# Value loads of a block-attention and soft-MoE kernel: two transfers on 128 partitions in place of eight on 32, with one more GpSimd copy

## The chip, the cores and the metric

The kernel runs on one NeuronCore of a Trainium2 chip. The metric is the device time of one execution, in microseconds (us). Five engines run side by side, each its own list of instructions in order: PE (TensorE, matmuls and transposes), DVE (VectorE), ACT (ScalarE), POOL (GpSimd) and SP (SyncE). SP does no arithmetic here; it issues every transfer between the chip's main memory and the on-chip memory of 128 partitions. [...]

## What is computed

Attention inside chunks of 64 tokens for 8 images of 8 heads, then a soft mixture of experts over all 4608 tokens:

```python
scores = scale * q_c @ k_c.T                  # per image, head and chunk of 64 tokens
attn = softmax(scores)
x = (attn @ v_c) -> (4608, 512)               # q, k, v: (8, 8, 576, 64) float32

logits = x @ phi                              # phi (512, 32)
d = softmax over tokens; c = softmax over slots
slot_out[e] = relu((d.T @ x)[e] @ w1[e]) @ w2[e]   # 8 experts, w1 (512, 1024), w2 (1024, 512)
out = c @ slot_out
```

## The kernel before

The 4608 tokens are worked off in nine blocks of 512 tokens, and each block in four units of two heads, so there are 36 units, t = 0 to 35. Eight of the blocks are the first 512 tokens of one image. The ninth (`b == NB - 1`) gathers the last 64 tokens of all eight images; it is fifth in order, so its units are t = 16 to 19.

For each unit SP loads keys and queries (`load_qk`, one transfer of 256 KB each, in the ninth block two of 128 KB each) into one of three buffers (`kn`, `qn`), five units ahead. Values are loaded for two units at once, that is, four heads (`load_v`, called when t is even, for units t+2 and t+3), into one of two buffers `vna` and `vnb`; together they are 512 KB. Before, these 512 KB go as eight transfers of 64 KB, each to 32 partitions. The weights `w1` and `w2` of the experts are loaded meanwhile in pieces of 512 KB (`load_pieces`), a little over one for each unit from t = 2 on.

A key or value row pair (tokens 2i and 2i+1, 512 bytes) lands on one partition. The matmul `values` wants something else: 64 keys of a chunk on 64 partitions, in both halves of a 128-column product, so `spread_v` on POOL copies one row of each pair to the other 32 partitions (two copies for each half of the partitions, `w` = 0 and 1, on 32 partitions of 256 elements each), and a memset sets the column of ones that gives the softmax sum. The even chunk (m = 0) of a pair of chunks lies on partitions `lo`, the odd one (m = 1) on `hi`. The eight transfers put the even chunk's pairs into columns 0 to 127 and the odd chunk's into columns 64 to 191 of each head's 194.

The loop over t writes the order of every engine by hand. In iteration t: weight pieces; scores of unit t; `spread_v(t)` on POOL; `values(t-1)` on PE; `load_v(t+2)` for even t; transposes of the keys and queries of unit t+1 (`turn_qk`); on POOL the pairing of heads of unit t+2 (`pair_heads`, two copies on 128 partitions of 512 elements); `load_qk(t+5)`; transposes of the outputs of unit t-2, and the logits and other block work at some iterations; at its end the transposes of the probabilities. POOL therefore runs spread, pair, pair for one unit after another, and a wait in `spread_v(t)` also holds the pairing for unit t+2. After the loop come a short tail of the last block, the experts (`up`, `turn`, `down`), and the outputs (`combine`, `store`).

SP issues in the order of the code. Each transfer signals one of eight semaphores, taken in rotation (shown below as DMAHW0 to DMAHW7), and it waits until the transfer that had the same semaphore before, eight places back, has landed; so at most eight transfers are under way. It also waits until its buffer is free.

Of the kernel before, what the change touches and what calls it, by code (L numbers as in the profile page):

```python
# [15 lines left out]
def kernel(  # L16
# [10 lines left out]
    nc = tc.nc  # L27
# [3 lines left out]
    B, H, S, D = q.shape  # L31
# [5 lines left out]
    TB = 512  # L37
    NB = B * S // TB
# [69 lines left out]
    with ExitStack() as actx:  # L108
# [6 lines left out]
        def tiles(name, n, shape):  # L115
            return [st.tile(shape, F32, name=f"{name}{i}") for i in range(n)]
# [6 lines left out]
        vn = tiles("vna", 1, [P, 2, 4, VW])  # L123
# [21 lines left out]
        def unit(t):  # L145
            n, hp = divmod(t, NHP)
            return n, order_b[n], hp
# [15 lines left out]
        def load_v(t):  # L163


            n, b, hp = unit(t)
            hs = slice(2 * hp, 2 * hp + 4)
            if b < NB - 1:
                src = v[b, hs, 0:TB].rearrange("a (M w m i u) d -> M w m i a (u d)", M=2, w=2, m=2, u=2)
            else:  # L170
                src = v[:, hs, TB:S].rearrange("(M w m) a (i u) d -> M w m i a (u d)", M=2, w=2, u=2)
            for M in range(2):
                for w in range(2):
                    for m in range(2):
                        p0 = 64 * w + 32 * m
                        nc.sync.dma_start(vn[t // 2 % 2][p0:p0 + 32, M, :, D * m:D * (m + 2)], src[M, w, m])  # L176

        def values_of(t):
            return vn[t // 2 % 2][:, :, 2 * (t % 2):2 * (t % 2) + 2]

        def spread_v(t):


            vv = values_of(t)
            for w in range(2):
                lo, hi = slice(64 * w, 64 * w + 32), slice(64 * w + 32, 64 * w + 64)
                nc.gpsimd.tensor_copy(vv[hi, :, :, 0:D], vv[lo, :, :, D:2 * D])  # L187
                nc.gpsimd.tensor_copy(vv[lo, :, :, 2 * D:3 * D], vv[hi, :, :, D:2 * D])  # L188
            nc.gpsimd.memset(vv[:, :, :, D:D + 1], 1.0)  # L189

# [218 lines left out]
        load_qk(0)  # L409
        load_qk(1)  # L410
        load_v(0)
        load_qk(2)
        nc.sync.dma_start(phi_sb, phi.rearrange("(f p) s -> p f s", p=P))
# [16 lines left out]
        for t in range(NT + 1):  # L430
# [5 lines left out]
            if t < NT:  # L436
                scores(t)
                s_sub(t)
                spread_v(t)
# [3 lines left out]
            if t % 2 == 0 and t + 2 < NT:  # L443
                load_v(t + 2)
# [227 lines left out]
```

## Time and profile before

| what | value |
|---|---|
| time, median of 3 runs (lowest to highest) | 308.19 us (305.33 to 310.34) |
| time of the profiled execution | 304.26 us |
| its span, first to last instruction | 302.5 us |
| busy share of PE, POOL, ACT, DVE | 74%, 36%, 41%, 41% |
| 16 DMA engines, busy share over the span | 79.3% (the SP queue) |
| mean granted PE clock | 0.891 |
| packets of the SP queue | 61776 |

The profile comes from one execution. A wait is the idle time of an engine just ahead of an instruction, put down to what released it last. "SPq" is SP issuing transfers; where it issues eight in one merged row, the row's length holds the waits between them as well. The DMA share of a short stretch can stand above 1, since packets overlap. The profiled execution is 3.9 us below the median of the runs.

### The profile page before, as it was taken

The page shows a single profiled execution, that of the slowest core. Times are in us where ns is not written, and L with a number is a line of the kernel's source. Part 1 is how long each engine was busy: PE and PEld are TensorE (multiplying, and loading weights), DVE is VectorE, ACT ScalarE, POOL GpSimd, SP SyncE. Part 2 cuts the span into 40 slices and gives each one's busy share as a digit, 9 for nine tenths or more (in the row PEclk, how much of TensorE's full clock was granted, in tenths as well). Part 3 has the DMA queues.
Part 4 walks back from the last instruction along what each step waited for, and adds up shares of the span by engine and source line. Part 5 has one row for each costly group of instructions (what it writes and reads, how often), then busy time and mean ns, then how long its engine had stood idle before and what let it go on. Part 6 is the DMA issues. An engine that isn't in the chain of part 4 may idle for free.

```text
span 302.5 us, 9554 instructions
## 1 busy us (share of the span) xinstructions
PE 222.6 (74%) x3828; PEld 165.6 (55%) x3828; DVE 122.9 (41%) x303; ACT 125.0 (41%) x277; POOL 108.7 (36%) x279
## 2 busy tenths in 40 slices
PE   8787859667784874979647787489576799998910
PEld 8666747557563653858437666376443224645800
DVE  0355534452743444274361656247453101025720
ACT  1467526453471554346543565356441011024610
POOL 2854552625435172543707437347310300000000
PEclk9999977997996899588995999989997699998675
DMA  7877958678695877868879687888689399968997
GB/s 189 243 179 194 278 160 226 207 195 258 178 251 153 231 203 205 264 165 215 239 194 288 190 228 232 223 230 263 141 286 407 119 335 361 347 213 292 316 321 298
DMA packets 61819, 71.99 MB, mean 238 GB/s; under 512 B 5456, under 2 KB 52560, under 8 KB 61776
## 3 DMA queue, kind: packets, MB, share of 16 engines
q1 hardware_dynamic: 61776, 71.39, 79.3%
q8 instruction: 30, 0.49, 0.7%
q14 instruction: 13, 0.11, 0.1%
HBM read 61.93 MB, written 9.44 MB: 236 GB/s over the span
## 4 chain that ended last, share of the span: by engine, by line
DMA 54%; PE 23%; POOL 6%; issue 4%; SPq 3%; DVE 2%; ACT 2%; POOLq 0%; ACTq 0%; DVEq 0%
DMA w<-in_moe_w_dram 29%; DMA vnb<-in_v_dram 14%; DMA vna<-in_v_dram 7%; PE ph L537 5%; PE pf L598 5%; PE po L571 5%; DMA qn<-in_q_dram 2%; PE pav L258 2%; SPq L154 2%; DMA knb<-in_k_dram 1%; SPq L176 1%; POOL vnb L188 1%; POOL vna L188 1%; POOL vnb L187 1%; POOL vna L187 1%
## 5 line engine op out<-in xcount | busy, mean ns | idle before, releaser
L216 ACT COPY kT<-pg 128x512 f32<-128x512 f32 x36 | 21.1, 586 | 80.2 <-PE pg L197 80.2
L232 DVE TENSOR_REDUCE mx<-psc 128x8 f32<-128x512 f32 x36 | 24.8, 689 | 45.9 <-PE psc L226 45.8
L258 PE MATMUL pav<-vnb,at 64*64 64x65 f32 x576 | 16.4, 247 | 26.2 <-POOL vnb L189 10.1
L187 POOL COPY vnb<-vnb 32x256 f32<-32x256 f32 x36 | 14.2, 394 | 50.7 <-DMA vnb<-in_v_dram 49.2
L247 ACT COPY at<-pt 128x512 f32<-128x512 f32 x36 | 21.1, 585 | 26.0 <-PE pt L244 26.0
L187 POOL COPY vna<-vna 32x256 f32<-32x256 f32 x36 | 14.2, 393 | 47.1 <-DMA vna<-in_v_dram 45.6
L197 PE MATMUL pg<-ident,kp 128*128 128x128 f32 x144 | 26.4, 312 | 4.3 <-DVE eT L336 4.3
L226 PE MATMUL psc<-kT,qT 64*64 64x64 f32 x1152 | 26.3, 229 | 4.4 <-issue 3.7
L258 PEld LDWEIGHTS pav<-vnb,at 64*64 64x64 f32 x576 | 13.7, 153 | 28.6 <-POOL vnb L189 24.2
L244 PE MATMUL pt<-ident,sc 128*128 128x128 f32 x144 | 24.8, 297 | 4.5 <-ACT sc L238 3.6
L226 PEld LDWEIGHTS psc<-kT,qT 64*64 64x64 f32 x1152 | 21.1, 139 | 11.2 <-issue 8.0
L197 PE MATMUL ph<-ident,qp 128*128 128x128 f32 x144 | 25.1, 302 | 2.2 <-issue 2.2
L258 PE MATMUL pav<-vna,at 64*64 64x65 f32 x576 | 15.0, 236 | 15.6 <-POOL vna L189 9.4
L233 DVE TENSOR_TENSOR sc<-psc,mx 128x512 f32<-128x512 f32 x36 | 24.9, 692 | 3.2
L273 DVE TENSOR_TENSOR xb<-pav,rc 128x512 f32<-128x512 f32 x36 | 24.9, 691 | 1.2
L244 PEld LDWEIGHTS pt<-ident,sc 128*128 128x128 f32 x144 | 17.1, 151 | 14.9 <-ACT sc L238 7.3
L279 PE MATMUL px<-ident,xb 128*128 128x128 f32 x144 | 24.6, 299 | 0.0
L238 ACT ACTIVATE sc<-sc 128x512 f32<-128x512 f32 x36 | 22.8, 633 | 0.6 <-DVE sc L233 0.6
L258 PEld LDWEIGHTS pav<-vna,at 64*64 64x64 f32 x576 | 12.6, 143 | 17.9 <-POOL vna L189 15.2
L193 POOL COPY qp<-qn 128x512 f32<-128x512 f32 x36 | 21.9, 609 | 0.1
L216 ACT COPY qT<-ph 128x512 f32<-128x512 f32 x36 | 20.7, 576 | 1.7 <-PE ph L197 1.7
L197 PEld LDWEIGHTS pg<-ident,kp 128*128 128x128 f32 x144 | 17.2, 155 | 7.6 <-issue 4.9
(94 smaller groups left out, 347.5 us busy)
## 6 DMA issues: line engine op xcount, KB each, us to landing
w<-in_moe_w_dram SPq DMA_DIRECT2D x64, 512.0 KB, 8.1
qn<-in_q_dram SPq DMA_DIRECT2D x32, 256.0 KB, 4.9
knb<-in_k_dram SPq DMA_DIRECT2D x21, 256.0 KB, 4.9
vna<-in_v_dram SPq DMA_DIRECT2D x72, 64.0 KB, 5.0
vnb<-in_v_dram SPq DMA_DIRECT2D x72, 64.0 KB, 5.6
out_dram<-ob SPq DMA_DIRECT2D x8, 512.0 KB, 3.7
out_dram<-ob SPq DMA_DIRECT2D x4, 1024.0 KB, 7.9
kna<-in_k_dram SPq DMA_DIRECT2D x11, 256.0 KB, 3.1
```

What stands on the lines that cost most here:

```text
L187: nc.gpsimd.tensor_copy(vv[hi, :, :, 0:D], vv[lo, :, :, D:2 * D])
L193: nc.gpsimd.tensor_copy(dst.rearrange("p j a d -> p a j d"), src)
L197: nc.tensor.transpose(out=dst[:, P * j:P * (j + 1)], in_=(kp if isk else qp)[:, j].rearrange("p a d -> p (a d)"), identity=ident)
L216: nc.scalar.copy(o, i)
L226: nc.tensor.matmul(psc[CH * m:CH * (m + 1), a, o:o + CH], lhsT=qT[r, c], rhs=kT[r, c], start=True, stop=True)
L232: nc.vector.reduce_max(mx, pv, axis=AX.X)
L233: nc.vector.tensor_tensor(sc.rearrange("p a M (w x) -> p a (M w) x", x=CH), pv, mx.unsqueeze(3).to_broadcast([P, 2, 4, CH]), ALU.subtract)
L238: nc.scalar.activation(sc, sc, AF.Exp, scale=SCALE)
L244: nc.tensor.transpose(out=pt[:, o:o + P], in_=sc[:, a, M], identity=ident)
L258: nc.tensor.matmul(pvv[q_, 2 * w + M, a, 0:D + 1], lhsT=at[r, a, M, q_], rhs=values_of(t)[r, M, a, 2 * D * m:2 * D * m + D + 1], start=Tru ...
L273: nc.vector.tensor_tensor(x_of(t).rearrange("p l (a d) -> p l a d", d=D), pvv[:, :, :, 0:D], rc.to_broadcast([P, 4, 2, D]), ALU.mult)
L279: nc.tensor.transpose(out=px[:, P * l:P * (l + 1)], in_=x_of(t)[:, l], identity=ident)
```

## The change

`load_v` loads the 512 KB of two units by two transfers of 256 KB on all 128 partitions, one for each group M of 256 tokens, all into columns 64 to 191. In the ninth block it issues eight transfers of 64 KB on 128 partitions, one for each M and head, whose source runs over four images and then 32 row pairs. Since every pair now lies in columns 64 to 191, `spread_v` first copies columns 64 to 127 to columns 0 to 63 on all partitions, and then makes the four copies of before, of which the first of each half reads other columns.

```diff
-            if b < NB - 1:
-                src = v[b, hs, 0:TB].rearrange("a (M w m i u) d -> M w m i a (u d)", M=2, w=2, m=2, u=2)
-            else:
-                src = v[:, hs, TB:S].rearrange("(M w m) a (i u) d -> M w m i a (u d)", M=2, w=2, u=2)
             for M in range(2):
-                for w in range(2):
-                    for m in range(2):
-                        p0 = 64 * w + 32 * m
-                        nc.sync.dma_start(vn[t // 2 % 2][p0:p0 + 32, M, :, D * m:D * (m + 2)], src[M, w, m])
+                dst = vn[t // 2 % 2][:, M, :, D:3 * D]
+                if b < NB - 1:
+                    nc.sync.dma_start(dst, v[b, hs, TB // 2 * M:TB // 2 * (M + 1)].rearrange(
+                        "a (p u) d -> p a (u d)", u=2))
+                else:
+                    for a in range(4):
+                        nc.sync.dma_start(dst[:, a], v[4 * M:4 * (M + 1), 2 * hp + a, TB:S].rearrange(
+                            "c (i u) d -> c i (u d)", u=2))
...
             vv = values_of(t)
+            nc.gpsimd.tensor_copy(vv[:, :, :, 0:D], vv[:, :, :, D:2 * D])
             for w in range(2):
                 lo, hi = slice(64 * w, 64 * w + 32), slice(64 * w + 32, 64 * w + 64)
-                nc.gpsimd.tensor_copy(vv[hi, :, :, 0:D], vv[lo, :, :, D:2 * D])
+                nc.gpsimd.tensor_copy(vv[hi, :, :, 0:D], vv[lo, :, :, 2 * D:3 * D])
                 nc.gpsimd.tensor_copy(vv[lo, :, :, 2 * D:3 * D], vv[hi, :, :, D:2 * D])
             nc.gpsimd.memset(vv[:, :, :, D:D + 1], 1.0)
```

On SP, around the second load into `vnb` (units 6 and 7), the order before is this; L154 loads keys or queries, L103 a weight piece, L176 values, and the brackets name the semaphores that the transfer waits for:

```order
L103 DMA w_0_1_439<-in_moe_w_dram 128x1024 [waits DMAHW5_49]
L176 DMA vnb_94<-in_v_dram 32x4x128 [waits DMAHW6_49,PE_49]
L176 DMA vnb_94<-in_v_dram 32x4x128 [waits DMAHW7_49,PE_49]
L176 DMA vnb_94<-in_v_dram 32x4x128 [waits DMAHW0_49]
L176 DMA vnb_94<-in_v_dram 32x4x128 [waits DMAHW1_49,PE_49]
L176 DMA vnb_94<-in_v_dram 32x4x128 [waits DMAHW2_49,PE_49]
L176 DMA vnb_94<-in_v_dram 32x4x128 [waits DMAHW3_49,PE_49]
L176 DMA vnb_94<-in_v_dram 32x4x128 [waits DMAHW4_49]
L176 DMA vnb_94<-in_v_dram 32x4x128 [waits DMAHW5_49,PE_49]
L154 DMA kna_87<-in_k_dram 128x2x256 [waits DMAHW6_49,Pool_49]
L154 DMA qn_84<-in_q_dram 128x2x256 [waits DMAHW7_49,Pool_49]
```

Of the change, the same place on SP, from the weight piece ahead of the values to the next load of values, two units later:

```order
L103 DMA w_0_1_425<-in_moe_w_dram 128x1024 [waits DMAHW3_49]
L171 DMA vnb_94<-in_v_dram 128x4x128 [waits DMAHW4_49,PE_49]
L171 DMA vnb_94<-in_v_dram 128x4x128 [waits DMAHW5_49,PE_49]
L154 DMA kna_87<-in_k_dram 128x2x256 [waits DMAHW6_49,Pool_49]
L154 DMA qn_84<-in_q_dram 128x2x256 [waits DMAHW7_49,Pool_49]
L103 DMA w_0_1_425<-in_moe_w_dram 128x1024 [waits DMAHW0_49]
L154 DMA knb_98<-in_k_dram 128x2x256 [waits DMAHW1_49,Pool_49]
L154 DMA qn_85<-in_q_dram 128x2x256 [waits DMAHW2_49,Pool_49]
L103 DMA w_1_0_570<-in_moe_w_dram 128x1024 [waits DMAHW3_49]
L171 DMA vna_91<-in_v_dram 128x4x128 [waits DMAHW4_49,PE_49]
L171 DMA vna_91<-in_v_dram 128x4x128 [waits DMAHW5_49,PE_49]
```

Before, the last value transfer waits for the weight piece just ahead of the first. In the change two units issue eight transfers (two of values, two of keys, two of queries, two weight pieces), so a value transfer waits for the value transfer of two units earlier.

On POOL, the first unit of a pair before (L187 and L188 are the four copies, L193 the pairing of heads):

```order
L187 COPY vnb_94<-vnb_94 32x2x2x64 [waits DMAHW5_49,DMAHW1_49,Pool_49]
L188 COPY vnb_94<-vnb_94 32x2x2x64 [waits DMAHW6_49,DMAHW2_49]
L187 COPY vnb_94<-vnb_94 32x2x2x64 [waits DMAHW7_49,DMAHW3_49]
L188 COPY vnb_94<-vnb_94 32x2x2x64 [waits DMAHW4_49,DMAHW0_49]
L189 MEMSET vnb_94 128x2x2 [waits Pool_49]
L193 COPY kp<-knb_98 128x2x4x64 [waits PE_49]
```

and of the change (L185 is the new copy, L194 the pairing of heads):

```order
L185 COPY vnb_94<-vnb_94 128x2x2x64 [waits DMAHW6_49,DMAHW5_49]
L188 COPY vnb_94<-vnb_94 32x2x2x64 [waits Pool_49]
L189 COPY vnb_94<-vnb_94 32x2x2x64 [waits Pool_49]
L188 COPY vnb_94<-vnb_94 32x2x2x64
L189 COPY vnb_94<-vnb_94 32x2x2x64 [waits Pool_49]
L190 MEMSET vnb_94 128x2x2 [waits Pool_49]
L194 COPY kp<-knb_98 128x2x4x64 [waits DMAHW3_49,PE_49]
```

One copy on 128 partitions is added ahead of the four, which wait for it and partly for each other through POOL's own semaphore.

## Rows read from the trace of the kernel before

**Rows 1.** The page: chain that ended last, shares of the span by line

```profile
DMA w<-in_moe_w_dram 29%; DMA vnb<-in_v_dram 14%; DMA vna<-in_v_dram 7%; PE ph L537 5%; PE pf L598 5%; PE po L571 5%; DMA qn<-in_q_dram 2%; PE pav L258 2%; SPq L154 2%; DMA knb<-in_k_dram 1%; SPq L176 1%; POOL vnb L188 1%; POOL vna L188 1%; POOL vnb L187 1%; POOL vna L187 1%
```

**Rows 2.** Waits: engine, line, releaser: us in total, times, longest us

```profile
POOL vnb L187 <- DMA vnb<-in_v_dram: 49.2, 9, 7.5
...
POOL vna L187 <- DMA vna<-in_v_dram: 45.6, 8, 7.5
```

**Rows 3.** Waits of SP's own queue

```profile
SPq L176 <- DMA w<-in_moe_w_dram: 50.0, 34, 3.0
...
SPq L176 <- DMA qn<-in_q_dram: 9.7, 15, 1.0
```

**Rows 4.** Timeline of SP: start us, length us, line, transfer, how many

```profile
110.49 7.87 SPq L176 DMA_DIRECT2D vnb<-in_v_dram  x8
...
184.73 0.46 SPq L103 DMA_DIRECT2D w<-in_moe_w_dram  x1
185.28 6.80 SPq L176 DMA_DIRECT2D vnb<-in_v_dram  x8
192.17 0.39 SPq L154 DMA_DIRECT2D kna<-in_k_dram  x1
...
195.17 8.47 SPq L176 DMA_DIRECT2D vna<-in_v_dram  x8
```

**Rows 5.** Timeline of POOL: first copy of a pair of units, idle time ahead

```profile
9.80 0.39 POOL L187 COPY vna<-vna 32x256 f32<-32x256 f32 x1
...
28.81 0.39 POOL L187 COPY vna<-vna 32x256 f32<-32x256 f32 x1 [3.50 <-DMA vna<-in_v_dram]
...
93.64 0.39 POOL L187 COPY vnb<-vnb 32x256 f32<-32x256 f32 x1 [7.46 <-DMA vnb<-in_v_dram]
...
119.12 0.39 POOL L187 COPY vnb<-vnb 32x256 f32<-32x256 f32 x1 [6.03 <-DMA vnb<-in_v_dram]
...
193.77 0.39 POOL L187 COPY vnb<-vnb 32x256 f32<-32x256 f32 x1 [6.34 <-DMA vnb<-in_v_dram]
...
216.67 0.39 POOL L187 COPY vnb<-vnb 32x256 f32<-32x256 f32 x1 [5.43 <-DMA vnb<-in_v_dram]
```

**Rows 6.** Stretches: window, us, busy of PE PEld DVE ACT POOL; PEclk, DMA, GB/s

```profile
28.81:216.67 187.86, 136.91 (x2734) 111.69 (x2733) 87.98 (x213) 89.80 (x198) 87.70 (x218) 0.90 0.78 218
93.64:119.12 25.48, 18.37 (x363) 15.13 (x363) 12.50 (x30) 12.04 (x27) 11.71 (x29) 0.87 0.76 209
...
9.80:28.81 19.01, 15.29 (x338) 12.61 (x328) 10.78 (x22) 11.37 (x21) 11.36 (x28) 1.00 0.81 211
```

**Rows 7.** Stretches of one us: values alone under way, then mostly weights

```profile
37.00:38.00 1.00, 1.00 (x34) 0.81 (x32) 0.41 (x1) 0.94 (x2) 0.00 (x0) 1.00 0.95 159
188.00:189.00 1.00, 1.00 (x14) 0.83 (x12) 0.93 (x4) 0.73 (x2) 0.00 (x0) 1.00 1.08 394
```

**Rows 8.** Timeline of PE: the value products of two units in a row

```profile
182.76 0.85 PE L258 MATMUL pav<-vna,at 64*64 64x65 f32 x32 [1.29 <-POOL vna L189]
...
186.84 0.70 PE L258 MATMUL pav<-vna,at 64*64 64x65 f32 x32 [0.15 <-issue]
```

**Rows 9.** Timeline of POOL: end of one spread, and the pairing of heads

```profile
205.50 0.40 POOL L187 COPY vna<-vna 32x256 f32<-32x256 f32 x1
205.95 0.40 POOL L188 COPY vna<-vna 32x256 f32<-32x256 f32 x1
206.41 0.10 POOL L189 MEMSET vna<- 128x4 f32 x1
206.57 0.61 POOL L193 COPY kp<-knb 128x512 f32<-128x512 f32 x1
207.12 0.61 POOL L193 COPY qp<-qn 128x512 f32<-128x512 f32 x1
```

**Rows 10.** The page: packets of the SP queue, and issues to landing, us

```profile
q1 hardware_dynamic: 61776, 71.39, 79.3%
...
qn<-in_q_dram SPq DMA_DIRECT2D x32, 256.0 KB, 4.9
...
vnb<-in_v_dram SPq DMA_DIRECT2D x72, 64.0 KB, 5.6
```

## The prediction

> **What bounds the kernel now.** I read the chain that ended last first: half of the span is transfers, the weight pieces and the two value buffers ahead of all [rows 1]. That names the place, not the cause, since the chain follows whatever landed last. So I asked who waits for values: POOL does, in its first copy of a pair of units, 49.2 us in 9 waits for `vnb` and 45.6 us in 8 for `vna` [rows 2], 94.8 us in all or 5.6 us a pair. In the loop the idle time of POOL passes straight on to PE, whose value product waits for the memset at the end of the spread [rows 8].
>
> Why are values late? SP's own waits answer: the line that issues them waits 50.0 us in 34 waits for weight pieces to land and 9.7 us for queries [rows 3]. It isn't that these transfers need the weights; the eight semaphores are used in rotation, so the eight value transfers can leave only as the eight transfers ahead of them land. The timeline shows it: SP begins to issue `vnb` at 185.28, right behind a weight piece, and needs 6.80 us for eight [rows 4], where one issue takes 0.39 to 0.46 us. POOL's first copy starts at 193.77 [rows 5], 8.5 us after the first issue. Meanwhile keys, queries and weights for later units stand behind them in SP's list.
>
> Last, is there room? From 28.81 to 216.67 the DMA engines are 0.78 busy and PE is busy 136.91 of 187.86 us [rows 6]. Nothing is full. The loop is bound by how many transfers may be under way, in the form of the value wait.
>
> **The change, part by part.** The sum is made on the profiled execution, span 302.5 us.
>
> *Eight transfers become two.* Per pair of units SP then issues about eight transfers, so a value transfer waits for one that was issued a pair earlier and has long landed. What stays is the wait for the buffer, which the product of two units earlier frees. From that product to the one that needs the new values lie three products; even at the 4.08 us from one product to the next of a stretch without waits [rows 8] that is 12.2 us, of which the spread takes 2.3. A 256 KB transfer lands 4.9 us after issue now [rows 10], so values should come in time, and I expect both waits of rows 2 nearly gone in the 16 pairs of ordinary blocks.
>
> *What is late next.* Three things bound the new pair from below. PE: 136.91 us over the 15 pair intervals of the stretch is 9.1 us of work a pair [rows 6]. To it come gaps like the 0.15 us ahead of a product [rows 8]; I take four a pair, 0.6, so 9.7. DMA: 0.78 of 187.86 us is 146.5, or 9.8 us a pair at full share [rows 6]; but part of it is slow. While values alone are under way the queue moves 159 GB/s at a share of 0.95, where weights move 394 [rows 7], so 512 KB of values take 3.3 us. On all partitions they may take between 1.3 us (at 394) and 3.3 us, which puts DMA at 7.8 to 9.8 us. POOL: spread and two pairings take 0.45 x 4 + 0.16 + 0.55 + 0.61, 3.1 us a unit [rows 9], so 6.2 a pair, and 7.1 to 7.5 with the new copy. The pair is then bound by PE at 9.7, with DMA close. I take 10.0, a little above the larger, since two engines near their limits don't fit perfectly; bounds 9.3 and 11.3.
>
> [...]
>
> *Ordinary intervals.* First copies of pairs stand at 28.81 and 216.67 [rows 5], 15 intervals, 187.86 us. The two that end in the ninth block's values take 93.64 to 119.12, 25.48 us. The other 13 take 162.38, 12.5 each. At 10.0 they give 13 x 2.5 = 32.5 us; at 9.3, 41.6; at 11.3, 15.6.
>
> *The first two intervals*, 9.80 to 28.81, 19.01 us, carry hardly any weights. PE is busy 15.29 of it [rows 6]. I take 17, so 2 us gained; bounds 0 and 3.7.
>
> *The ninth block.* There the count stays eight, so the eight-semaphore hold stays as it is (7.87 us for the `vnb` of units 18 and 19, [rows 4]), and nothing is gained. New is the source: it runs over four images first, then 32 row pairs, where each old transfer ran over 32 row pairs first. The trace has no transfer with so short an outer dimension. If it is shared out as before, the cost is 0. If four pieces mean four of 16 engines, 512 KB go over a quarter of the engines. At the value rate, 159/0.95/16 = 10.5 GB/s an engine, that is 12.5 us instead of 3.1 to 3.3, 9.3 more a pair or 19 in two; at the weights' rate, 394/1.08/16 = 22.8 GB/s, 5.7 us, 5 more in two. The engines are idle for 0.24 of 25.48, 6 us, which can take some of it. I take 5, with bounds 0 and 19.
>
> [...]
>
> *The new copy and its waits on POOL.* The copy works on 256 elements of 128 partitions; the trace has 0.40 for 256 elements on 32 partitions and 0.61 for 512 on 128 [rows 9]; I take 0.40, bounds 0.40 and 0.61. A wait for POOL's own previous instruction, as the memset has now, leaves 0.06 us [rows 9], so three new ones cost at most 0.2. Together 0.5 a unit, 18 us of work in 36 units. On the path this costs nothing, because POOL then works 7.1 to 7.5 of 10 us. If that cover were gone (values still late), 0.5 to 0.8 a pair, 9 to 14 us in 17 pairs, would be added.
>
> *Fewer issues and packets.* SP issues 96 transfers less; SP waits and isn't short of time, so 0. After 216.67 nothing of the change is left, and the 85.8 us to the end stay.
>
> **Sum:** 302.5 - 32.5 - 2 + 5 = 273 us of span. The median of the runs stands 3.9 us above the profiled execution's 304.26, so the same saving of 29.5 gives 308.2 - 29.5 = 279 us.
>
> **Rivals.**
>
> A, the forecast: 279, within 266 to 290 (pairs of 9.3 to 10.8 us, the ninth block 0 to 8). For it: rows 3 show the hold, and no engine is full. 0.62.
>
> B, the wait moves to other transfers: POOL then waits for values or keys as long as before in part, because DMA reaches no more than about 0.87 of a stretch. Then a pair takes 9.8/0.87 = 11.3 us, and the saving is 15.6 + 1 - 5 = 11.6, time 297. Against it: single microseconds with weights reach more than 1 [rows 7]. 0.14.
>
> C, the ninth block is confined to four engines at the slow rate and nothing is hidden: 32.5 + 2 - 19 = 15.5 saved, 293. For it: an outer count of four is new here, and no row excludes the loss. Against its full size: the 6 us that the engines idle there, and the faster of the two prices. 0.12. [...]
>
> D, no gain: the transfers are what is slow, not their number under way. Intervals of 12.3 save 3, the ninth block takes 5 back: 310. Rows 3 speak against it. 0.08.
>
> E, slower: the ninth block's transfers, taken apart badly, run on one engine. At 10.5 GB/s 512 KB take 50 us a pair, 47 more, 94 in two: 308 - 34 + 94 = 368. It decides from a loss of 41 us on (34.5 plus 2%), about 24 us a pair for 512 KB, or two engines. 0.04.
>
> **How the numbers follow.** A measurement of this kernel can tell about 2% from no change. Faster by more than 2% (below 302) holds in A and C and nearly all of B: 0.87. Within 2%: D, and the rest of B: 0.09. Slower: E, 0.04. The range runs from A's lower end, 266, to B's and C's side, 298, and leaves out D and E and a little at either end, about 0.18.
>
> **What would show it.** SP should show two value issues of under 1 us in place of rows of 7 to 9 us; the waits of rows 2 should fall from 94.8 to under 20 us, what remains standing at units 16 and 18; first copies of ordinary pairs should stand 10 us apart; the DMA share of the stretch should rise to about 0.9. Packets: by the shapes of all transfers 56832 pieces of data are moved, and the other 4944 of the 61776 [rows 10] are 16 for each of 309 transfers; 96 transfers fewer give 60240, and if the ninth block's 16 close with four each, 192 less again, 60048. The forecast is wrong if POOL still waits 3 us or more for values in ordinary pairs, if the intervals stay above 11.3, or if the ninth block's two intervals exceed 40 us together.

## The result and the profile after

The changed kernel takes 263.92 us (median of 4 runs, 263.51 to 264.51); the kernel before, timed beside it, 309.26 us (4 runs, 305.33 to 313.81). The ratio is 0.8605, with a 95% interval of 0.8531 to 0.8679: 14% faster. The forecast was faster, 279 us; the time lies 15 us below it and 2 us below the lower end of the range, 266. The profiled execution took 264.01 us, with a span of 262.2 us. Of two kernels below (`eight128`, `eight32`) and of `best` and `skipw_again` the profiled execution was one of the longer ones; the ratios leave such runs out, and rows of these kernels are read here for what happens, not for the last microsecond.

The waits for values, the lines that answer to [rows 2] (POOL's first instruction of a pair is now L185), are these; columns as there:

```profile
POOL vna L185 <- DMA vna<-in_v_dram: 17.7, 7, 4.5
...
POOL vnb L185 <- DMA vnb<-in_v_dram: 11.6, 5, 6.5
```

29.3 us in place of 94.8. SP's own waits answer to [rows 3]:

```profile
SPq L154 <- POOL kp L194: 37.4, 21, 2.5
...
SPq L171 <- PE pav L259: 7.9, 5, 4.3
...
SPq L175 <- DMA w<-in_moe_w_dram: 0.4, 1, 0.4
```

The line that issues values no longer waits 50 us for weight pieces to land; SP now waits for POOL to free a key buffer, which is what it should wait for in a loop that runs ahead. The timeline of SP in the changed kernel (start, length, line, transfer, how many) has two issues of an ordinary block, and above them both loads of the ninth block:

```profile
74.75 5.94 SPq L175 DMA_DIRECT2D vna<-in_v_dram  x8
...
86.67 7.97 SPq L175 DMA_DIRECT2D vnb<-in_v_dram  x8
...
135.69 0.93 SPq L171 DMA_DIRECT2D vna<-in_v_dram  x2
```

0.93 us against 6.80 to 8.47 in [rows 4]; the eight of the ninth block still take 5.94 and 7.97 us.

First copies of pairs on POOL, as in [rows 5]:

```profile
10.05 0.39 POOL L185 COPY vna<-vna 128x256 f32<-128x256 f32 x1
...
26.57 0.40 POOL L185 COPY vna<-vna 128x256 f32<-128x256 f32 x1 [2.24 <-DMA vna<-in_v_dram]
...
72.15 0.40 POOL L185 COPY vnb<-vnb 128x256 f32<-128x256 f32 x1 [2.70 <-DMA vnb<-in_v_dram]
...
97.27 0.40 POOL L185 COPY vnb<-vnb 128x256 f32<-128x256 f32 x1 [6.53 <-DMA vnb<-in_v_dram]
...
108.86 0.40 POOL L185 COPY vna<-vna 128x256 f32<-128x256 f32 x1 [4.46 <-DMA vna<-in_v_dram]
...
169.49 0.40 POOL L185 COPY vnb<-vnb 128x256 f32<-128x256 f32 x1
```

From 26.57 to 169.49 there are 15 intervals, 142.92 us; the two that end in the ninth block's values (72.15 to 97.27) take 25.12, the other 13 take 117.80, 9.06 each in place of 12.49. The stretches, with the columns of [rows 6]:

```profile
26.57:72.15 45.58, 41.10 (x896) 32.48 (x896) 29.14 (x71) 29.65 (x64) 32.86 (x83) 1.00 1.00 306
72.15:97.27 25.12, 19.15 (x435) 14.69 (x433) 14.61 (x34) 15.06 (x36) 13.21 (x33) 1.00 0.65 185
108.86:161.00 52.14, 46.23 (x1045) 36.05 (x1037) 34.16 (x81) 33.91 (x76) 39.66 (x99) 1.00 0.97 309
```

In ordinary blocks the DMA share is 0.97 to 1.00 at 306 to 309 GB/s, where the whole stretch before had 0.78 and 218; the granted PE clock is 1.00 where it was 0.90. Over all 15 intervals, like for like, they are now 0.90, 281 GB/s and 0.98. In the ninth block's intervals the share is 0.65.

### The profile page after: what moved, and what is told of

It reads as the page before. It is cut to its first block, busy times and chain, and to the rows that moved or that the text cites. A ratio compares the mean times of both kernels' runs of the same rounds, so it can differ in the third digit from the quotient of the medians.

```text
span 262.2 us, 9367 instructions
## 1 busy us (share of the span) xinstructions
PE 211.6 (81%) x3828; PEld 151.6 (58%) x3828; DVE 123.6 (47%) x303; ACT 124.9 (48%) x277; POOL 122.2 (47%) x315
## 2 busy tenths in 40 slices
DMA packets 60090, 71.97 MB, mean 274 GB/s; under 512 B 3728, under 2 KB 50832, under 8 KB 60048
## 3 DMA queue, kind: packets, MB, share of 16 engines
q1 hardware_dynamic: 60048, 71.38, 85.5%
## 4 chain that ended last, share of the span: by engine, by line
PE 46%; DMA 12%; POOL 11%; ACT 11%; DVE 9%; issue 5%; SPq 1%; ACTq 0%; POOLq 0%; DVEq 0%
PE ph L538 6%; PE po L572 5%; PE pf L599 5%; PE pt L245 5%; PE pg L198 4%; PE pav L259 4%; DMA vna<-in_v_dram 4%; ACT sc L239 3%; PE psc L227 3%; PE pg L290 3%; DMA qn<-in_q_dram 3%; DMA knb<-in_k_dram 3%; PE ph L143 3%; ACT kT L217 2%; DMA vnb<-in_v_dram 2%
## 5 line engine op out<-in xcount | busy, mean ns | idle before, releaser
L198 PE MATMUL pg<-ident,kp 128*128 128x128 f32 x144 | 23.5, 287 | 6.1 <-DVE eT L337 4.1
L198 PE MATMUL ph<-ident,qp 128*128 128x128 f32 x144 | 22.4, 279 | 0.2 <-issue 0.2
L280 PE MATMUL px<-ident,xb 128*128 128x128 f32 x144 | 22.2, 278 | 0.0
L259 PE MATMUL pav<-vnb,at 64*64 64x65 f32 x576 | 13.7, 229 | 10.4 <-POOL vnb L190 5.7
L194 POOL COPY qp<-qn 128x512 f32<-128x512 f32 x36 | 22.0, 612 | 0.2 <-DMA qn<-in_q_dram 0.2
L198 PEld LDWEIGHTS pg<-ident,kp 128*128 128x128 f32 x144 | 15.4, 142 | 9.4 <-issue 3.8
L259 PEld LDWEIGHTS pav<-vnb,at 64*64 64x64 f32 x576 | 11.3, 138 | 12.8 <-POOL vnb L190 6.0
L194 POOL COPY kp<-knb 128x512 f32<-128x512 f32 x24 | 14.7, 611 | 8.3 <-PE pg L198 6.4
L280 PEld LDWEIGHTS px<-ident,xb 128*128 128x128 f32 x144 | 17.1, 143 | 1.0 <-ACT xTa L283 0.8
L198 PEld LDWEIGHTS ph<-ident,qp 128*128 128x128 f32 x144 | 17.0, 143 | 1.0 <-POOL vna L188 0.4
L538 PE MATMUL ph<-w,siT 128*32 128x512 f32 x128 | 17.2, 692 | 0.0
```

The costliest lines, as they stand in the source:

```text
L194: nc.gpsimd.tensor_copy(dst.rearrange("p j a d -> p a j d"), src)
L198: nc.tensor.transpose(out=dst[:, P * j:P * (j + 1)], in_=(kp if isk else qp)[:, j].rearrange("p a d -> p (a d)"), identity=ident)
L259: nc.tensor.matmul(pvv[q_, 2 * w + M, a, 0:D + 1], lhsT=at[r, a, M, q_], rhs=values_of(t)[r, M, a, 2 * D * m:2 * D * m + D + 1], start=Tru ...
L280: nc.tensor.transpose(out=px[:, P * l:P * (l + 1)], in_=x_of(t)[:, l], identity=ident)
L538: nc.tensor.matmul(ph[SL * i:SL * (i + 1), :], lhsT=siT[:, j, :], rhs=wt[1, e, j // 2][:, j % 2, DM * h:DM * (h + 1)], start=(j == 0), sto ...
```

## The experiments

Medians are given with the ratio to the kernel before, timed on the same chip; the sets ran on different chips, so ratios are compared across sets, and a difference of two ratios is given in us of the kernel before (309).

### Count or partitions

`eight128` loads ordinary blocks by eight transfers again, each on 128 partitions:

```diff
-                    nc.sync.dma_start(dst, v[b, hs, TB // 2 * M:TB // 2 * (M + 1)].rearrange(
-                        "a (p u) d -> p a (u d)", u=2))
+                    for a in range(4):
+                        nc.sync.dma_start(dst[:, a], v[b, 2 * hp + a, TB // 2 * M:TB // 2 * (M + 1)].rearrange(
+                            "(p u) d -> p (u d)", u=2))
```

> Ordinary blocks load the values of two units by eight transfers again, but each on 128 partitions (one group M and one head, 64 KB); layout, new copy and ninth block as in the changed kernel. Theory 1, the number of transfers under way is what bound the kernel before: SP's waits in the value line come back (50 us and more in total), pairs take 11 to 12.5 us, time 290 to 310. Theory 2, the 32 partitions were the cause: pairs stay at 9 to 10 us, time 264 to 275.

294.09 us, ratio 0.953 (0.944 to 0.962). Of the waits, POOL's for values and SP's own in the value line (L172 here):

```profile
POOL vna L187 <- DMA vna<-in_v_dram: 36.4, 7, 8.9
POOL vnb L187 <- DMA vnb<-in_v_dram: 34.2, 9, 6.4
```

```profile
SPq L172 <- DMA w<-in_moe_w_dram: 37.7, 29, 2.5
```

The same layout, the same new copy, the same partitions, and the wait behind weight pieces is back, with 70.6 us of waits for values. So the count is what bound the kernel: by the ratios (0.953 against 0.8605) about 29 of the 43 us saved return with it. The size of one transfer goes with the count (64 KB for 256 KB); that SP waits again for pieces to land says that the hold is what costs. Theory 1 holds in direction and time; 37.7 us is less than the 50 it named.

`eight32` undoes the transfers altogether (eight on 32 partitions in all blocks, into the new columns) and keeps the new copy:

```diff
+                    for c in range(4):
+                        r0 = TB // 2 * M + 64 * c
+                        nc.sync.dma_start(dst[32 * c:32 * (c + 1)], v[b, hs, r0:r0 + 64].rearrange(
+                            "a (i u) d -> i a (u d)", u=2))
```

> All blocks load values by eight transfers on 32 partitions as in the kernel before, into the columns of the changed kernel, with the new copy kept: the transfers are undone and the copy alone stays. Theory 1, the copy lies in the path when values are late: 17 pairs x 0.5 us more than before, time 314 to 320. Theory 2, the copy is hidden even there: 306 to 311. If neither count nor partitions mattered, it would stay near 264.

307.82 us, ratio 0.988 (0.979 to 0.997). The copy costs nothing that can be seen even where values are late; theory 1, 0.5 us a pair in the path, falls. Against `eight128`, on the same chip and with the same count, 32 partitions cost 3.5% more by the ratios, about 11 us (the ninth block differs as well, which `ninth32` below shows to make no difference to the time). So both halves of the change matter: count about 29 us, partitions about 11.

`four128` and `four64` load ordinary blocks by four transfers of 128 KB, on 128 or on 64 partitions:

```diff
# four128
+                    for g in range(2):
+                        nc.sync.dma_start(dst[:, 2 * g:2 * g + 2], v[b, 2 * hp + 2 * g:2 * hp + 2 * g + 2,
+                                                                     TB // 2 * M:TB // 2 * (M + 1)].rearrange(
+                            "a (p u) d -> p a (u d)", u=2))
# four64
+                    for w in range(2):
+                        r0 = TB // 2 * M + TB // 4 * w
+                        nc.sync.dma_start(dst[64 * w:64 * (w + 1)], v[b, hs, r0:r0 + TB // 4].rearrange(
+                            "a (p u) d -> p a (u d)", u=2))
```

> Ordinary blocks load the values of two units by four transfers of 128 KB on 128 partitions (group M, two heads). Theory 1, the count under way decides: two units then issue ten transfers where eight may be under way, so a value transfer waits for something issued most of a pair ago; a partial loss between 264 (two transfers) and 294 (eight), 266 to 280. Theory 2, only the eight that fill the whole rotation hurt: 263 to 266.

> Ordinary blocks load values by four transfers of 128 KB on 64 partitions each, against four on 128 partitions, 263.4 us. Theory 1, fewer partitions make a value transfer slower at equal count: with PE's chain now the bound, most of it is hidden, 264 to 270. Theory 2, partitions do not matter: 262 to 265.

`four128`: 263.4 us, ratio 0.856 (0.847 to 0.865), no loss against two transfers. `four64`: 275.88 us, ratio 0.890 (0.883 to 0.897), 3.4% or about 10 us slower at the same count and size. The same stretch of both and the SP queue over the whole span (packets, MB, share), `four128` first:

```profile
26.60:72.00 45.40, 39.58 (x888) 31.18 (x887) 28.14 (x69) 29.31 (x63) 31.83 (x80) 1.00 0.95 291
```

```profile
q1 hardware_dynamic: 60560, 71.38, 85.5%
```

```profile
26.60:72.00 45.40, 38.13 (x816) 30.73 (x815) 26.45 (x66) 27.02 (x59) 30.57 (x77) 0.96 1.07 279
```

```profile
q1 hardware_dynamic: 60560, 71.38, 92.9%
```

The DMA share is higher and less is moved. The same packets and bytes take 92.9% of a span of 274.2 us on 64 partitions and 85.5% of 260.2 on 128, 255 and 222 us of queue time. The two kernels also cut the source differently (four heads of 128 tokens, or two heads of 256, in one transfer); that was not tested apart from the partitions, here or between `eight128` and `eight32`. For `four128` theory 2 holds: two units then issue ten transfers, and the hold falls on keys and queries, which are loaded five units ahead: SP waits 14.3 us for weight pieces in their line (L154) and 1.2 us in the value line. For `four64` theory 1 was right on the cause, but the time lies 6 us above its range: less is hidden than I thought, since the DMA queue has little room left (share 0.95 in the stretch of `four128`).

### What bounds the new pair

`noweights` moves all weight pieces of the loop behind it:

```diff
-            want = min(2 * NWA, 2 * NWA * max(t - 1, 0) // (NT - 5))
-            load_pieces(wpa, want - (2 * nload - len(pieces)))
...
+        load_pieces(wpa, 2 * NWA)
         turn_x(NT - 1)
```

> The changed kernel with all weight pieces of the loop issued behind the loop; the total time rises by the later loads, and only the loop's pairs are read. Theory 1, the ordinary pairs are now held by DMA throughput (share 0.97 to 1.00): without weights they fall from 8.7 to 9.1 us to 8.4 or less and the DMA share to 0.6 or 0.7. Theory 2, PE and its chain hold them: they stay at 8.6 us or more.

277.47 us in a single run, of which only the loop counts. Timeline of PE, the value products four units (one block) apart, of `noweights` and then of the changed kernel:

```profile
102.71 0.70 PE L259 MATMUL pav<-vna,at 64*64 64x65 f32 x32 [0.15 <-POOL vna L185]
...
120.86 0.70 PE L259 MATMUL pav<-vna,at 64*64 64x65 f32 x32 [0.15 <-POOL vna L185]
```

```profile
48.26 0.69 PE L259 MATMUL pav<-vna,at 64*64 64x65 f32 x32 [0.15 <-POOL vna L188]
...
66.41 0.69 PE L259 MATMUL pav<-vna,at 64*64 64x65 f32 x32 [0.15 <-POOL vna L185]
```

Both blocks take 18.15 us, 9.07 a pair. A stretch of `noweights`:

```profile
100.00:150.00 50.00, 45.20 (x1012) 35.32 (x1010) 33.94 (x84) 33.40 (x76) 36.51 (x93) 1.00 0.61 182
```

With the DMA share at 0.61 the pair is no shorter, so PE and what it waits for between its products hold it: theory 2. PE is busy 0.904 of the time at a granted clock of 1.00, 8.2 us of a pair's 9.07. That the DMA share in the changed kernel is 1.00 as well means that the two limits lie next to each other; `four64` shows the other one taking over (DMA share 1.07, PE busy 38.13 of 45.40 us).

### The copy

`nocopy` leaves the new copy out from unit 4 on:

```diff
-            nc.gpsimd.tensor_copy(vv[:, :, :, 0:D], vv[:, :, :, D:2 * D])
+            if t < 4:
+                nc.gpsimd.tensor_copy(vv[:, :, :, 0:D], vv[:, :, :, D:2 * D])
```

> The new copy on GpSimd is left out from unit 4 on (columns 0 to 63 of the lower partitions keep older values; a part of the spread is not computed). Theory 1, the copy is hidden behind GpSimd's idle time: 262.5 to 264.5. Theory 2, with pairs of 8.7 to 9.1 us the 7.1 us of GpSimd and its late start put it in the path: 32 units x 0.45 us at most, 250 to 260.

263.7 us, ratio 0.857 (0.850 to 0.864), where `four128`, which keeps the copy, has 0.856 on the same chip and the changed kernel 0.856 and 0.861. No difference: the copy is hidden.

### The ninth block

`ninth32` gives each of its eight transfers one image (32 partitions, four heads):

```diff
-                    for a in range(4):
-                        nc.sync.dma_start(dst[:, a], v[4 * M:4 * (M + 1), 2 * hp + a, TB:S].rearrange(
-                            "c (i u) d -> c i (u d)", u=2))
+                    for c in range(4):
+                        nc.sync.dma_start(dst[32 * c:32 * (c + 1)], v[4 * M + c, hs, TB:S].rearrange(
+                            "a (i u) d -> i a (u d)", u=2))
```

> The ninth block alone is changed: its eight transfers of 64 KB take one image each (32 partitions, four heads) in place of one head of four images (128 partitions). Count of transfers and everything else stay. Theory 1, the outer count of four confines a transfer to a quarter of the engines: the SP queue's packets rise from 60048 to 60240, POOL's waits for the values of units 16 and 18 (4.0 and 6.5 us) shrink, and the time falls by 3 to 10 us, to 254 to 261. Theory 2, the hold by eight semaphores alone makes these two pairs slow: packets may rise, but the time stays within 1.5 us of 264.

263.62 us, ratio 0.855 (0.846 to 0.863): no difference. The packets of the SP queue, of the changed kernel and of `ninth32`, with the columns of [rows 10]:

```profile
q1 hardware_dynamic: 60048, 71.38, 85.5%
```

```profile
q1 hardware_dynamic: 60240, 71.38, 85.9%
```

192 packets more, 12 for each of 16 transfers, as forecast for transfers that close with four packets in place of sixteen. That they run on four engines the count doesn't show. The time doesn't tell the two forms apart. But `ninth32` gives up 128 partitions for 32 as well, so it shows only that the two forms cost the same, not that an outer count of four costs nothing. In `ninth32` the pair of units 18 and 19 waits as before:

```profile
96.28 0.40 POOL L186 COPY vnb<-vnb 128x256 f32<-128x256 f32 x1 [6.38 <-DMA vnb<-in_v_dram]
```

`wafter` moves the weight pieces of an iteration behind the values:

```diff
-            want = min(2 * NWA, 2 * NWA * max(t - 1, 0) // (NT - 5))
-            load_pieces(wpa, want - (2 * nload - len(pieces)))
...
             if t % 2 == 0 and t + 2 < NT:
                 load_v(t + 2)
+            want = min(2 * NWA, 2 * NWA * max(t - 1, 0) // (NT - 5))
+            load_pieces(wpa, want - (2 * nload - len(pieces)))
```

> The changed kernel with one line moved: the weight pieces of an iteration are issued behind the values and not ahead of them. Theory 1, in the ninth block the eight semaphores hold the values behind a weight piece, and elsewhere values queue behind it: POOL's waits for values fall from 29 us to under 15, the intervals that end at units 16 and 18 shrink from 11.1 and 14.0 us by 2 to 4 each, time 252 to 260. Theory 2, DMA throughput is what the loop waits for: the order of transfers changes nothing, 262 to 266.

262.19 us, ratio 0.852 (0.846 to 0.858); `four128`, with the order unchanged, had 0.856 on the same chip. POOL's waits for values:

```profile
POOL vnb L185 <- DMA vnb<-in_v_dram: 8.2, 2, 6.3
...
POOL vna L185 <- DMA vna<-in_v_dram: 6.7, 2, 3.9
```

They halve, as theory 1 said, and the time moves by a microsecond or two at most: in ordinary blocks the waits that are left on POOL mostly don't hold PE. In the changed kernel PE waited 7.9 us in all for the memset of a spread, 5.6 of it at once. The 6.3 us of the ninth block remain.

The trace says what this wait holds. Stretches in which the last values of units 18 and 19 are under way, of `wafter`, the changed kernel and `noweights`:

```profile
90.00:94.00 4.00, 2.79 (x74) 2.12 (x72) 2.26 (x6) 3.12 (x9) 0.00 (x0) 1.00 0.30 76
```

```profile
92.00:96.00 4.00, 2.12 (x68) 1.61 (x60) 1.93 (x5) 2.45 (x8) 0.00 (x0) 1.00 0.30 79
```

```profile
84.00:88.00 4.00, 3.71 (x101) 3.07 (x97) 2.60 (x6) 2.74 (x6) 3.33 (x9) 1.00 0.28 73
```

For four microseconds the queue works at a share of about 0.30 and moves 73 to 79 GB/s, near the 0.25 that four of sixteen engines would give; that it is four is my estimate. In the first two POOL does nothing and PE runs out of work; in the third, without weight pieces, the same stretch comes early enough and PE stays busy. So these transfers are slow, and behind weight pieces they are late enough for it to be felt.

`skipw` issues no weight piece in iterations 13 to 16 and spreads the 34 over the rest; `best` does this, the order of `wafter` and the transfers of `ninth32` together:

```diff
-            want = min(2 * NWA, 2 * NWA * max(t - 1, 0) // (NT - 5))
+            want = min(2 * NWA, -(-2 * NWA * sum(x not in (13, 14, 15, 16) for x in range(2, t + 1)) // 30))
```

> The changed kernel with no weight piece issued in iterations 13 to 16; the 34 pieces are spread over the other iterations of the loop (2 to 35). Theory 1, the ninth block is slow because its many transfers wait in the rotation of eight semaphores behind weight pieces: POOL's wait of 6.5 us for unit 18 shrinks to under 3, products of units 14 and 20 stand 28 to 31 us apart in place of 36.4, time 255 to 260. Theory 2, it is slow because each transfer runs on four engines: the 36.4 stay and the time is 262 to 266.

> The three edits together: weight pieces behind the values, none in iterations 13 to 16, and the ninth block's values in eight transfers of one image each, which spread over all engines. Theory 1: units 14 to 20 take 28 us as without weights, time 253 to 257. Theory 2, the ninth block has too many transfers in any case: 258 to 262.

`skipw`: 259.77 us, ratio 0.838 (0.831 to 0.845). `best`: 260.86 us, ratio 0.843 (0.8375 to 0.8485) on the same chip, so the two further edits add nothing to the time; that lies in the range of theory 2, too many transfers in any case, though not far above that of theory 1, 257. Value products of units 14 and 20, timeline of PE, of the changed kernel (the first of the 32 matmuls of unit 14) and of `skipw`:

```profile
74.91 0.24 PE L259 MATMUL pav<-vnb,at 64*64 64x65 f32 x1 [0.15 <-issue]
...
111.31 0.70 PE L259 MATMUL pav<-vna,at 64*64 64x65 f32 x32 [0.73 <-POOL vna L190]
```

```profile
77.32 0.70 PE L259 MATMUL pav<-vnb,at 64*64 64x65 f32 x32 [0.15 <-issue]
...
106.00 0.70 PE L259 MATMUL pav<-vna,at 64*64 64x65 f32 x32 [0.89 <-POOL vna L190]
```

36.4 us become 28.7, as theory 1 of `skipw` said, and POOL's wait for unit 18 falls from 6.5 to 1.9 us (put down to keys there). Without any weight piece, in `noweights`, it is 27.9 us (its product of unit 20 is shown above, at 102.71), as many as six units of ordinary blocks (22 to 28) take there:

```profile
74.83 0.91 PE L259 MATMUL pav<-vnb,at 64*64 64x65 f32 x32 [0.15 <-issue]
...
111.21 0.70 PE L259 MATMUL pav<-vnb,at 64*64 64x65 f32 x32 [0.15 <-issue]
...
139.01 0.69 PE L259 MATMUL pav<-vna,at 64*64 64x65 f32 x32 [0.15 <-POOL vna L185]
```

So the ninth block is slow because of the weight pieces among its many transfers: 8.5 us of the changed kernel's loop go there. With the pieces away, the low share costs PE nothing; with them there, late values take the four microseconds shown above to land, and no run here loads the ninth block on all partitions by transfers with a larger outer count. How much of the 8.5 us is the hold in the rotation and how much the DMA time of the pieces is not separated either; `wafter`, which changes only the order, takes 33.5 us from unit 14 to unit 20. In `best` POOL's waits for values are gone (0.8 us in all) and 14 to 20 take about 30 us, yet the time doesn't follow: unit 14 comes 5.9 us later there than in the changed kernel.

Since the two kernels had been timed on different chips, they ran once more side by side.

> The changed kernel, timed again on the chip on which the next kernel is timed: 262 to 266, as before.

> No weight piece in iterations 13 to 16, beside the changed kernel on one chip. Theory 1, the ninth block's transfers wait behind weight pieces in the rotation: 3 to 6 us below the changed kernel. Theory 2, the earlier difference came from the chip: within 1.5 us of it.

261.87 us, ratio 0.856 (0.848 to 0.864), just under the range expected, and 260.70 us, ratio 0.840 (0.829 to 0.852). Value products of units 14, 20 and 35 (the last), of the changed kernel (of unit 14 the first matmul again) and of `skipw`:

```profile
75.15 0.24 PE L259 MATMUL pav<-vnb,at 64*64 64x65 f32 x1 [0.15 <-POOL kp L194]
...
111.80 0.70 PE L259 MATMUL pav<-vna,at 64*64 64x65 f32 x32 [0.15 <-POOL kp L194]
...
178.82 0.70 PE L259 MATMUL pav<-vnb,at 64*64 64x65 f32 x32 [0.78 <-issue]
```

```profile
77.79 0.70 PE L259 MATMUL pav<-vnb,at 64*64 64x65 f32 x32 [0.15 <-issue]
...
109.36 0.70 PE L259 MATMUL pav<-vna,at 64*64 64x65 f32 x32 [0.15 <-POOL vna L185]
...
177.45 0.70 PE L259 MATMUL pav<-vnb,at 64*64 64x65 f32 x32 [0.78 <-issue]
```

From unit 14 to unit 20 it is 5.1 us less again (36.7 to 31.6). Most of it is given back: unit 14 comes 2.6 us later, and units 20 to 35 take 1.1 us more. In the first pair of traces unit 14 came 2.4 us later and the end took 2.8 more, so the loop gains 1.4 and 2.5 us as a whole. That fits the weight pieces, which now come in ordinary blocks where the DMA share is 0.97 to 1.00 in the changed kernel; it is argued, not tested. How much better `skipw` is, by 1 us (medians) or by 5 (ratios), is not settled; the intervals overlap.

## Why the prediction was right or wrong

**Right: the cause.** The hold by eight transfers, more than bandwidth, bound the loop. `eight128` brings hold and most of the time back with layout, copy and partitions unchanged. Rival D (the transfers themselves are slow) is part of the truth, though: `eight32` against `eight128` and `four64` against `four128` put 10 to 11 us on the number of partitions. I had that only as a lower price of DMA time, which I thought would stay hidden.

**Wrong in size: the pair.** I took 10.0 us, from 9.1 us of PE work, 0.6 us of gaps and some room. The measured pair is 9.06 (9.07 from product to product). The step that failed is the price of PE's work: 136.91 us over 15 pairs was read in a stretch with a mean granted clock of 0.90 [rows 6], that is, partly at a much lower one. For instance, POOL waits 5.92 us for values up to 41.08, PE does nothing from 41 to 43, and then (before, POOL and a stretch):

```profile
41.08 0.39 POOL L187 COPY vnb<-vnb 32x256 f32<-32x256 f32 x1 [5.92 <-DMA vnb<-in_v_dram]
```

```profile
43.00:49.00 6.00, 5.96 (x78) 5.51 (x82) 1.12 (x4) 2.19 (x5) 4.00 (x9) 0.50 0.87 283
```

The granted clock is 0.50 there. In the ordinary blocks of the changed kernel it is 1.00, and the same work takes 8.2 us a pair (41.10 of 45.58 us); 136.91 x 0.90 / 15 is 8.2 too. The one long wait that is left shows it again: behind the 6.53 us at 97.27 the granted clock is 0.71 up to 108.86. I priced the work at a mean that holds stretches at 0.50 behind such waits, and the change removes most of the waits. With 8.2 + 0.9 of gaps the sum would have met the pair. My lower bound, 9.3, carried the same error and lay above the result. The lower end of the range doesn't even follow from it: 9.3 a pair, 2 us in the first intervals and nothing lost in the ninth block make 308.2 - 43.6 = 264.6, not 266. By first copies the 13 intervals give 44.6 us where I expected 32.5; about 4 of the 44.6 are no gain but POOL running ahead at the end, since from the first copy of unit 34 to the end it is 92.7 us now and 85.8 before, of which only 2.6 are real (last item).

**Wrong in size: the ninth block.** I charged 5 us, for transfers confined to four engines, which was a supposition. The two intervals take 25.12 us against 25.48: nothing lost, nothing gained. The packets (60048) and the DMA share (0.30) fit four engines, though neither shows the number, and the transfers are slow: at the 79 GB/s of 92 to 96 us, 512 KB take 6.6 us, between the two prices of the prediction. What it left out is that they replace transfers on 32 partitions, which `ninth32` shows to be no better there (263.62 us against 263.92). That the hold stays there, as the prediction said, fits `skipw`, where the loss goes with the weight pieces. Rival C named a confinement that fits the packets and the share, with a loss that isn't there against the kernel before; rival E needed more of it.

**Not every sign came.** The waits for values were to fall under 20 us, the rest at units 16 and 18. They fell to 29.3: 10.5 at these two, and 18.8 in ordinary pairs, of which units 20 (4.46) and 24 (3.75) passed the 3 us that the prediction named as a sign of being wrong. Little of that reaches PE (7.9 us, above). The DMA share of the stretch is 0.90, as forecast.

**Right: the first intervals and the copy.** 10.05 to 26.57 is 16.5 us against a forecast of 17. The copy takes 0.40 us and is hidden (`nocopy`, `eight32`).

**Wrong: the step from the profiled execution to the median.** I carried the 3.9 us by which the profiled execution of before lay under its median over to the changed kernel. That is 4 of the 15 us by which the forecast missed; the other 11 are in the span (273 against 262.2). With the runs taken since, the gap of before is 5.0 us (309.26 to 304.26); the changed kernel has none (263.92 and 264.01). So the medians differ by 45.3 us where the profiled spans differ by 40.3. The runs of before spread over 8.5 us, those of the changed kernel over 1.0 (3.5 in `after_again`); where one execution falls in such a spread is in part luck, and why the spread of before is wide was not tested.

**Not foreseen: 2.6 us lost behind the loop.** I had said that nothing changes there. From the last value product to the end it is 81.0 us before (221.50 to 302.50) and 83.6 after (178.56 to 262.20). Part of it is the first group of expert matmuls, 64 in each, timeline of PE before and after:

```profile
236.72 8.75 PE L537 MATMUL ph<-w,siT 128*32 128x512 f32 x64
```

```profile
194.13 9.93 PE L538 MATMUL ph<-w,siT 128*32 128x512 f32 x64
```

Over these stretches the granted clock is 0.82 and 0.72 (windows 236.7 to 246.0 and 194.1 to 204.6). Why it rises later in the one than in the other was not tested.

The account in spans: 0.25 lost at the start, 2.5 gained in the first intervals, 44.6 in the ordinary ones, 0.4 in the ninth block, 6.9 lost after the last first copy; together 40.3, which is 302.5 - 262.2.

## What to carry to other kernels

Where an issuing engine waits in the line that issues many small transfers, count how many may be under way and how many the program issues between two uses of one buffer: here eight of eight against two of eight was worth about 29 of 43 us, and four was as good as two. Give transfers all 128 partitions; at equal count and bytes 32 or 64 cost 10 to 11 us here. A part that stays slow can be slow only together with what is issued around it: the ninth block lost 8.5 us with weight pieces among its transfers, and none without. When a wait is taken away, price the work that remains at the clock of a stretch without such waits (here 1.00 against a mean of 0.90, 8.2 us of PE work a pair against 9.1), and don't carry the run-to-run offset of the waiting kernel over.

## What the runs showed of the hardware that was not expected

The 16 transfers of the ninth block whose source has an outer count of four have 12 packets fewer each than those of `ninth32` (60048 against 60240). While such transfers alone are under way, the DMA share is 0.28 to 0.30 and 73 to 79 GB/s are moved, where the values alone of the kernel before, on 32 partitions, had 0.95 and 159 [rows 7]; that this is four engines of 16 is my estimate from 0.30 and the packets. In the time of the kernel it can't be told from transfers on 32 partitions whose source runs over 32 row pairs first (263.92 and 263.62 us).

Transfers on 64 partitions take more of the queue's time than on 128: 279 GB/s at a DMA share of 1.07 against 291 at 0.95, and 255 against 222 us for the 71.38 MB of the whole span, with pieces of 512 bytes in both. So the pieces of 512 bytes are ruled out as the cause of the difference; why fewer partitions take longer was not shown.

A GpSimd copy of 256 elements takes 0.40 us on 128 partitions and 0.39 to 0.40 on 32 [rows 5] [rows 9], and 512 elements take 0.61 us: the partitions cost nothing here, the elements do.
